# Linear attention and soft mixture of experts in one kernel: fewer and larger transfers, other homes in the arena, and two half experts moved

## Chip, cores and metric

The kernel runs on one core of a Trainium2 chip. The metric is the device time of one execution in microseconds (us); the times shown are medians of runs. TensorE does the matrix products (PE in the profile, PEld its weight loads), VectorE is DVE, ScalarE is ACT, GpSimd is POOL. SyncE (SP) issues every transfer of this kernel, on one queue that 16 DMA engines serve in the order of issue.

## What is computed

```python
kv = einsum('bhsd,bhse->bhde', k, v)              # 8 batches, 8 heads, 576 tokens, 64 wide
out = einsum('bhsd,bhde->bhse', q, kv)
x = out / sqrt(mean(out*out, -1) + 1e-6) * g_norm # 4608 tokens x 512 after the heads are joined
logits = x @ phi                                  # 4608 x 32 slots
d = softmax of logits over tokens; slot_input = d.T @ x     # 32 x 512
for e in range(8):                                # 4 slots per expert
    slot_out[e] = relu(slot_input[e] @ w1[e]) @ w2[e]       # 512 -> 1024 -> 512
return softmax of logits over slots @ slot_out    # 4608 x 512
```

All is float32. The weights w1 and w2 are 16 MB each, q, k and v 9 MB each, the result 9 MB.

## The kernel before

**Memory.** One tile, `arena`, holds all that is loaded and stored: 160 places of 256 floats for each of 128 partitions, behind a small head. `KV_AT` gives the places of k and v of each batch (18 places each), `Q_AT` those of q of each pair of batches (18), `W_AT` those of the units of w1 and w2 (16 each), `OUT_AT` those of the 12 output chunks (6 each). A place is used several times: a load into it has to wait until the last reader of what stood there is done. Unit 7 of w1 goes into `xall`, the tile that held x.

**Loads.** SP issues them in the order of the program. `load_head`, `load_row` and `load_w` are one transfer each. `W_ROWS` says which units of w1 and w2 lie side by side in memory and come in one transfer; `load_w` of a row's first member loads the row. A transfer has one completion: who needs a part of it waits for the whole. The q of pair 1 comes in two parts, `load_head(4, 0, 2048)` and `load_head(4, 2048, TOK)`.

**First stage.** `for T in range(NT - 2)` walks 36 tiles of 128 tokens, with the last two written out behind it. A batch's k and v products (`Kv.products`, line 205, `borders`, line 220) are made three steps ahead of the first tile that needs them (`kv_steps`): batch 2 at T = 6 to 8, batch 3 at T = 10 to 12, batch 4 at T = 15 to 17, batch 6 at T = 24 to 26. `products(T)` (line 273) is o = q times kv, together with its part of the logits; ScalarE squares and copies it out, VectorE, ScalarE and GpSimd make the norm and the logits, and `group_sum` (line 422) adds to the slot inputs with a running maximum. `loads_behind` names the loads that are issued behind a given T. TensorE takes all this in the order written.

**Second stage.** `fill` puts products of zeros where TensorE would otherwise stand still. Then come the experts: `expert_h(e)` (line 636) multiplies by w1, `expert_y(e, hf)` (line 654) by one half of w2's columns, so that output half 0 can leave while half 1 is still computed. Units 0 and 1 of w2 hold both halves of experts 0 and 1. For the later six, units 2, 3, 4 hold half 0 of experts 2 and 3, 4 and 5, 6 and 7, and units 5, 6, 7 half 1 of the same. `combine(k)` is the softmax over slots for a third of the tokens, on VectorE and ScalarE. `gather(hf)` copies the sum over experts from PSUM (line 670), `mix(hf)` adds its four parts by a product and copies it (z, line 676). `output(hf, k, f)` makes one of 12 chunks by four products (line 687), copied by ScalarE (line 695) and VectorE (line 697), and when the last chunk of an entry of `OUT_ROWS` is copied, SP issues that entry's transfer (line 701).

The order of half 0 and half 1 before: after `expert_h(7)`, `expert_y` of experts 2 to 7 for half 0, `gather(0)`, half of expert 0 for half 1, `mix(0)`, the other half, two chunks, experts 1 to 3, a chunk, experts 4 and 5, two chunks, experts 6 and 7, `gather(1)`, the sixth chunk, `mix(1)`, six chunks.

Of the kernel before, what the change touches and what calls it, by code (L numbers as in the profile page):

```python
# [14 lines left out]
P = 128  # L15
# [3 lines left out]
NE = 8  # L19
# [10 lines left out]
LATE_FILL = (16, 3, 3, 1, 1)  # L30
# [11 lines left out]
}  # L42
W_ROWS = (
    (("w1", 0, None), ("w2", 0, None)),
    (("w1", 1, None), ("w2", 1, None)),
    (("w1", 2, None), ("w1", 3, None)),
    (("w1", 4, None), ("w2", 2, 1)),
    (("w1", 5, None),),
    (("w1", 6, None),),
    (("w1", 7, None),),  # L50
    (("w2", 2, 0),),
    (("w2", 3, None),),
    (("w2", 4, None),),
    (("w2", 5, None),),
    (("w2", 6, None),),
    (("w2", 7, None),),
)
OUT_AT = (16, 22, 28, 34, 40, 46, 72, 128, 134, 78, 84, 90)
OUT_ROWS = ((0, 1), (2, 3), (4, 5), (6,), (7, 8), (9, 10, 11))
# [11 lines left out]
def soft_moe_linear_attention(ctx: ExitStack, tc: tile.TileContext, first_in, head_in, t2_in, kv5_in, t3_in, w_in, out):  # L71
# [13 lines left out]
    def place(at, n):  # L85
        return arena[:, HEAD + at * KB : HEAD + at * KB + n]

    def load_head(u, lo, hi):
        at = (KV_AT[0], KV_AT[1], Q_AT[0], KV_AT[2], Q_AT[1], KV_AT[3])[u]
        nc.sync.dma_start(place(at, TOK)[:, lo:hi], head_in[u, :, lo:hi])  # L90

    def load_row(at, src):
        nc.sync.dma_start(place(at, src.shape[-1]), src)
# [30 lines left out]
    def w_block(kind, u, i):  # L124
# [7 lines left out]
    load_head(0, 2304, TOK)  # L132
    load_head(2, 0, 2048)
    load_head(1, 0, 2304)
    load_head(1, 2304, TOK)
    load_head(2, 2048, TOK)
    load_head(3, 0, TOK)
    load_head(4, 0, 2048)
# [5 lines left out]
        21: lambda: load_w("w1", 1),  # L144
        26: lambda: load_w("w1", 2),
        27: lambda: load_w("w1", 4),
        31: lambda: load_w("w1", 5),
# [334 lines left out]
    load_head(5, 0, TOK)  # L482
    load_head(4, 2048, TOK)
    load_row(KV_AT[4], t2_in)
    load_row(KV_AT[5], kv5_in)
# [72 lines left out]
    load_w("w1", 6)  # L558
    load_w("w1", 7)
    load_w("w2", 2, 0)  # L560
# [151 lines left out]
    load_w("w2", 5)  # L712
    expert_y(1, 0)
    combine(1)
    for e in range(3, NE):
        expert_h(e)
        if e == 4:
            load_w("w2", 6)
            combine(2)
        if e == 5:  # L720
            load_w("w2", 7)
    for e in range(NE - LATE, NE):
        expert_y(e, 0)
    chunks = [(k, f) for k in range(NCH) for f in range(2)]
    gather(0)
    expert_y(0, 1, range(4))
    mix(0)
    expert_y(0, 1, range(4, 8))
    output(0, *chunks[0])
    output(0, *chunks[1])  # L730
    expert_y(1, 1)
    expert_y(2, 1)
    expert_y(3, 1)
    output(0, *chunks[2])
    expert_y(4, 1)
# [12 lines left out]
def build_program():  # L748
    import concourse.bacc as bacc

    nc = bacc.Bacc("TRN2", target_bir_lowering=False, num_devices=1, dynamic_dma_scratch_size=SCRATCH)
    shapes = {
        "first": (P, HEAD + 2304), "head": (6, P, TOK), "t2": (P, 2 * TOK), "kv5": (P, TOK), "t3": (P, 3 * TOK),
        "w": (1, 2 * NE * P * UNIT),
    }
    args = [nc.dram_tensor(f"in_{n}_dram", s, F32, kind="ExternalInput").ap() for n, s in shapes.items()]
    args.append(nc.dram_tensor("out_0_dram", (1, 4 * NCH * P * 4 * CT * NS), F32, kind="ExternalOutput").ap())
    with tile.TileContext(nc, schedule_with_timeline_sim=True) as tc, tc.manual_schedule():
        soft_moe_linear_attention(tc, *args)
    return nc  # L760
# [56 lines left out]
```

## Time and profile before

| | |
|---|---|
| median of three runs | 175.05 us (174.93 to 175.15) |
| the profiled execution | 175.01 us, its span 173.2 us |
| TensorE products / weight loads busy | 148.8 us / 107.2 us |
| VectorE / ScalarE / GpSimd busy | 87.2 / 87.2 / 57.2 us |
| mean granted TensorE clock | 0.967 |
| moved by all queues | 71.67 MB, mean 414 GB/s |

The span is the time from the first to the last instruction that the profile shows; the execution is 1.8 us longer. In a row of instructions the first number is the start in us from the span's beginning, the second the time taken; `x32` is the number of instructions merged into the row, and the bracket says how long the engine stood idle before and who ended that. In a row of transfers stand the KB moved and the us from issue to landing. In a row of stretches stand each engine's busy time, the granted clock, the share of the DMA engines and GB/s.

### The profile page before, as it was taken

The page shows a single profiled execution, that of the slowest core. Times are in us where ns is not written, and L with a number is a line of the kernel's source. Part 1 is how long each engine was busy: PE and PEld are TensorE (multiplying, and loading weights), DVE is VectorE, ACT ScalarE, POOL GpSimd, SP SyncE. Part 2 cuts the span into 40 slices and gives each one's busy share as a digit, 9 for nine tenths or more (in the row PEclk, how much of TensorE's full clock was granted, in tenths as well). Part 3 has the DMA queues.
Part 4 walks back from the last instruction along what each step waited for, and adds up shares of the span by engine and source line. Part 5 has one row for each costly group of instructions (what it writes and reads, how often), then busy time and mean ns, then how long its engine had stood idle before and what let it go on. Part 6 is the DMA issues. An engine that isn't in the chain of part 4 may idle for free.

```text
span 173.2 us, 4657 instructions
## 1 busy us (share of the span) xinstructions
PE 148.8 (86%) x1973; PEld 107.2 (62%) x1973; DVE 87.2 (50%) x184; ACT 87.2 (50%) x224; POOL 57.2 (33%) x68
## 2 busy tenths in 40 slices
PE   7688988999999899999999989899996499978500
PEld 2467967889689888888896773456663235433200
DVE  1112266383677464757725988526885033456600
ACT  2026586787956888869679760213221031315500
POOL 6000338558356575482765488000000000000000
PEclk9969999999999999999999999999999999999955
DMA  5999999999999998999999999999999999999994
GB/s 197 416 432 431 439 404 446 408 492 417 395 417 489 491 409 358 424 429 435 416 431 422 439 395 426 431 416 422 429 422 424 428 424 424 394 397 410 430 447 192
DMA packets 4628, 71.67 MB, mean 414 GB/s; under 512 B 512, under 2 KB 512, under 8 KB 640
## 3 DMA queue, kind: packets, MB, share of 16 engines
q1 hardware_dynamic: 4608, 71.38, 97.2%
q8 instruction: 15, 0.25, 0.6%
q14 instruction: 5, 0.04, 0.1%
HBM read 61.94 MB, written 9.44 MB: 412 GB/s over the span
## 4 chain that ended last, share of the span: by engine, by line
PE 50%; DMA 24%; ACT 7%; DVE 6%; issue 3%; SPq 2%; POOL 1%; POOLq 1%; DVEq 0%
PE o L273 19%; DMA arena<-in_head_dram 13%; DMA arena<-in_w_dram 11%; PE kvp_kv L205 8%; PE po L687 6%; PE pY L654 6%; PE pS L422 3%; PE ph L636 2%; PE o L264 2%; DVE arena L697 2%; SPq L90 1%; ACT arena L695 1%; ACT sq L283 1%; PE kvp_kv L220 1%; ACT xall L291 1%
## 5 line engine op out<-in xcount | busy, mean ns | idle before, releaser
L273 PE MATMUL o<-bd,arena 128*128 128x192 f32 x256 | 49.3, 336 | 1.9 <-ACT bd L250 1.1
L273 PEld LDWEIGHTS o<-bd,arena 128*128 128x128 f32 x256 | 40.8, 190 | 5.2 <-ACT bd L250 1.6
L296 DVE TENSOR_REDUCE ms<-sq 128x16 f32<-128x1024 f32 (+1 forms) x19 | 22.1, 1163 | 28.7 <-ACT sq L283 28.4
L323 POOL TENSOR_TENSOR xall<-xall,r 128x512 f32<-128x512 f32 x34 | 34.8, 1044 | 0.0
L345 POOL TENSOR_TENSOR part<-part,r 128x512 f32<-128x512 f32 x17 | 17.8, 1048 | 49.4 <-DVE r L314 49.4
L283 ACT ACTIVATE sq<-o 128x512 f32<-128x512 f32 x36 | 21.5, 598 | 10.9 <-PE o L273 10.5
L291 ACT COPY xall<-o 128x512 f32<-128x512 f32 x34 | 20.6, 607 | 0.0
L695 ACT COPY arena<-po 128x768 f32<-128x768 f32 x12 | 9.3, 800 | 22.0 <-PE po L687 21.9
L654 PE MATMUL pY<-arena,xall 128*32 128x256 f32 x256 | 15.8, 381 | 3.8 <-DMA arena<-in_w_dram 3.3
L205 PE MATMUL kvp_kv<-arena 128*64 128x64 f32 x480 | 17.2, 225 | 2.1 <-DMA arena<-in_first_dram 1.1
L205 PEld LDWEIGHTS kvp_kv<-arena 128*64 128x64 f32 x480 | 15.2, 138 | 5.6 <-DMA arena<-in_first_dram 2.0
L358 DVE TENSOR_REDUCE logits<-part 128x64 f32<-128x512 f32 (+1 forms) x18 | 17.8, 991 | 0.0
L697 DVE COPY arena<-po 128x768 f32<-128x768 f32 x12 | 11.3, 956 | 10.6 <-PE po L687 10.6
L687 PE MATMUL po<-logits,z 32*128 32x384 f32 x96 | 13.5, 525 | 2.1 <-DVE z L676 0.9
L654 PEld LDWEIGHTS pY<-arena,xall 128*32 128x32 f32 x256 | 8.0, 109 | 11.1 <-issue 4.8
L636 PE MATMUL ph<-arena,sTe 128*32 128x256 f32 x224 | 12.7, 379 | 0.3 <-DVE sTe L583 0.3
L290 ACT COPY part<-o 128x256 f32<-128x256 f32 x34 | 12.6, 370 | 0.0
L422 PE MATMUL pS<-xall,d 128*32 128x129 f32 x288 | 10.8, 277 | 1.2 <-ACT d L410 1.1
L687 PEld LDWEIGHTS po<-logits,z 32*128 32x128 f32 x96 | 5.8, 183 | 8.9 <-ACT arena L695 5.0
L636 PEld LDWEIGHTS ph<-arena,sTe 128*32 128x32 f32 x224 | 7.2, 110 | 5.3 <-DVE sTe L583 0.7
L422 PEld LDWEIGHTS pS<-xall,d 128*32 128x32 f32 x288 | 7.2, 109 | 4.4 <-issue 3.9
L465 PE MATMUL fill<-zeros 128*128 128x512 bf16 x26 | 8.3, 476 | 1.1 <-DVE zeros L157 1.1
(93 smaller groups left out, 139.3 us busy)
## 6 DMA issues: line engine op xcount, KB each, us to landing
arena<-in_w_dram SPq DMA_DIRECT2D x7, 2048.0 KB, 21.1
arena<-in_w_dram SPq DMA_DIRECT2D x3, 4096.0 KB, 24.7
arena<-in_t_dram SPq DMA_DIRECT2D x1, 6912.0 KB, 36.6
out_dram<-arena SPq DMA_DIRECT2D x4, 1536.0 KB, 7.1
arena<-in_head_dram SPq DMA_DIRECT2D x2, 2304.0 KB, 23.0
arena<-in_t_dram SPq DMA_DIRECT2D x1, 4608.0 KB, 36.5
arena<-in_head_dram SPq DMA_DIRECT2D x3, 1152.0 KB, 12.0
arena<-in_w_dram SPq DMA_DIRECT2D x1, 3072.0 KB, 27.9
```

The costliest lines, as they stand in the source:

```text
L205: nc.tensor.matmul(self.pkv[lo : lo + 64, w, g], lhsT=main[:, w, 1, c, lo : lo + 64], rhs=main[:, w, 0, c, lo : lo + 64], start=c == 0 and ...
L273: nc.tensor.matmul(o[:, r, :192], lhsT=q_main(2 * g + i)[:, r, at : at + P], rhs=bds[i][:, r], start=True, stop=True)
L283: nc.scalar.activation(sqs[s][:, T - starts[s]], o[:, :, 32:160], AF.Square, scale=0.125)
L291: nc.scalar.copy(xts[T % NX][:, :, :128], o[:, :, 32:160])
L296: nc.vector.tensor_reduce(out=mss[s], in_=sqs.pop(s).rearrange("p t j (w d) -> p (t j w) d", w=2), axis=AX.X, op=ALU.add)
L323: nc.gpsimd.tensor_tensor(out=x, in0=x, in1=r[:, i].rearrange("p (j w) -> p j w", w=2).unsqueeze(3).to_broadcast([P, 4, 2, D]), op=ALU.mult,)
L345: engine.tensor_tensor(out=part, in0=part, in1=rs_of[s].unsqueeze(3).to_broadcast([P, STAGES[s], H, NS]), op=ALU.mult)
L358: nc.vector.tensor_reduce(out=L[:, pos(starts[s]) : pos(starts[s]) + STAGES[s]], in_=parts.pop(s).rearrange("p t h n -> p t n h"), axis=AX ...
L422: nc.tensor.matmul(pS[32 * j : 32 * j + 32], lhsT=ds[G][:, i], rhs=x[:, j], start=i == 0, stop=i == GROUPS[G] - 1)
L636: nc.tensor.matmul(ph[32 * j : 32 * j + 32], lhsT=sTe[:, (4 * e + c) * NS : (4 * e + c + 1) * NS], rhs=w_block("w1", e, 4 * c + j), start= ...
L654: nc.tensor.matmul(pY[32 * j : 32 * j + 32, hf, :256], lhsT=hTs[e][:, c], rhs=w_block("w2", u, at + c), start=e == 0 and c < 4, stop=e == ...
L687: nc.tensor.matmul(po[:, u, : CT * NS].rearrange("p (g x) -> p g x", g=2), lhsT=z[lo : lo + 32, f * P : (f + 1) * P], rhs=cT[k][lo : lo + 32],
```

## The change

Transfers are joined and moved. The second half of the first batch's k and v, q of pair 0 and batch 1 are loaded as before. Batch 2's k and v come in one transfer with the first part of q of pair 1; the rest of q of pair 1 with batch 4's k and v; q of pair 2 with batch 5's. Units 0 and 1 of w1 become one row; units 0 and 1 of w2 join unit 4 of w1 and half 1 of unit 2 of w2 (behind T = 27); half 0 of unit 2 of w2, unit 6 and unit 5 of w1 become one row, issued where unit 6 was; units 3 and 4 of w2 one row, units 5 and 6 another. The row with units 2 and 3 of w1 moves from T = 26 to T = 25, and the row that stood ahead of it (units 1 of w1 and w2, T = 21) is gone. Unit 1 of w1, units 0, 4 and 6 of w2 and all output chunks get other homes. The seventh, eighth and ninth chunk leave in one transfer, so that outputs are five transfers and not six. In the second stage, half 1 of experts 0 and 1 is computed ahead of experts 4 to 7 of half 0, with four fill products behind it, and the chunks of half 0 are placed anew.

```diff
-LATE_FILL = (16, 3, 3, 1, 1)
+LATE_FILL = (16, 3, 3, 1, 1, 4)
...
 W_AT = {
-    ("w1", 0): (72,), ("w2", 0): (88,), ("w1", 1): (128,), ("w2", 1): (144,), ("w1", 2): (0,),
+    ("w1", 0): (72,), ("w1", 1): (88,), ("w2", 0): (128,), ("w2", 1): (144,), ("w1", 2): (0,),
     ("w1", 3): (16,), ("w1", 4): (104,), ("w1", 5): (56,), ("w1", 6): (40,), ("w1", 7): None,
-    ("w2", 2): (32, 120), ("w2", 3): (72,), ("w2", 4): (128,), ("w2", 5): (0,), ("w2", 6): (104,), ("w2", 7): (56,),
+    ("w2", 2): (32, 120), ("w2", 3): (72,), ("w2", 4): (88,), ("w2", 5): (0,), ("w2", 6): (16,), ("w2", 7): (56,),
 }
 W_ROWS = (
-    (("w1", 0, None), ("w2", 0, None)),
-    (("w1", 1, None), ("w2", 1, None)),
+    (("w1", 0, None), ("w1", 1, None)),
     (("w1", 2, None), ("w1", 3, None)),
-    (("w1", 4, None), ("w2", 2, 1)),
-    (("w1", 5, None),),
-    (("w1", 6, None),),
+    (("w1", 4, None), ("w2", 2, 1), ("w2", 0, None), ("w2", 1, None)),
+    (("w2", 2, 0), ("w1", 6, None), ("w1", 5, None)),
     (("w1", 7, None),),
-    (("w2", 2, 0),),
-    (("w2", 3, None),),
-    (("w2", 4, None),),
-    (("w2", 5, None),),
-    (("w2", 6, None),),
+    (("w2", 3, None), ("w2", 4, None)),
+    (("w2", 5, None), ("w2", 6, None)),
     (("w2", 7, None),),
 )
-OUT_AT = (16, 22, 28, 34, 40, 46, 72, 128, 134, 78, 84, 90)
-OUT_ROWS = ((0, 1), (2, 3), (4, 5), (6,), (7, 8), (9, 10, 11))
+OUT_AT = (32, 38, 44, 50, 104, 110, 116, 122, 128, 134, 140, 146)
+OUT_ROWS = ((0, 1), (2, 3), (4, 5), (6, 7, 8), (9, 10, 11))
...
     nc.sync.dma_start(arena[:, : HEAD + 2304], first_in)
-    load_head(0, 2304, TOK)
-    load_head(2, 0, 2048)
-    load_head(1, 0, 2304)
-    load_head(1, 2304, TOK)
-    load_head(2, 2048, TOK)
-    load_head(3, 0, TOK)
-    load_head(4, 0, 2048)
+    load_row(KV_AT[0] + 9, kv_in[0, :, 2304:])
+    load_row(Q_AT[0], q0_in[:, :2048])
+    load_row(KV_AT[1], kv_in[1, :, :2304])
+    load_row(KV_AT[1] + 9, kv_in[1, :, 2304:])
+    load_row(Q_AT[0] + 8, q0_in[:, 2048:])
+    load_row(KV_AT[2], kv2_in)
 
     loads_behind = {
         9: lambda: load_row(KV_AT[6], t3_in),
         18: lambda: load_w("w1", 0),
-        21: lambda: load_w("w1", 1),
-        26: lambda: load_w("w1", 2),
+        25: lambda: load_w("w1", 2),
         27: lambda: load_w("w1", 4),
-        31: lambda: load_w("w1", 5),
     }
...
-    load_head(5, 0, TOK)
-    load_head(4, 2048, TOK)
-    load_row(KV_AT[4], t2_in)
-    load_row(KV_AT[5], kv5_in)
+    load_row(KV_AT[3], kv_in[2])
+    load_row(Q_AT[1] + 8, kv4_in)
+    load_row(Q_AT[2], kv5_in)
...
-    load_w("w1", 6)
+    load_w("w2", 2, 0)
     load_w("w1", 7)
-    load_w("w2", 2, 0)
...
     expert_h(0)
+    expert_h(1)
     load_w("w2", 3)
-    expert_h(1)
-    load_w("w2", 4)
     expert_y(0, 0)
     combine(0)
     expert_h(2)
-    load_w("w2", 5)
     expert_y(1, 0)
     combine(1)
     for e in range(3, NE):
         expert_h(e)
+        if e == 3:
+            load_w("w2", 5)
         if e == 4:
-            load_w("w2", 6)
             combine(2)
         if e == 5:
             load_w("w2", 7)
-    for e in range(NE - LATE, NE):
+    expert_y(2, 0)
+    expert_y(3, 0)
+    expert_y(0, 1)
+    expert_y(1, 1)
+    fill(LATE_FILL[5], home=ps.tile([P, 2, 512], F32, tag="m", name="fill")[:, 0], cols=512)
+    for e in range(4, NE):
         expert_y(e, 0)
     chunks = [(k, f) for k in range(NCH) for f in range(2)]
     gather(0)
-    expert_y(0, 1, range(4))
     mix(0)
-    expert_y(0, 1, range(4, 8))
     output(0, *chunks[0])
     output(0, *chunks[1])
-    expert_y(1, 1)
+    output(0, *chunks[2])
     expert_y(2, 1)
     expert_y(3, 1)
-    output(0, *chunks[2])
+    output(0, *chunks[3])
     expert_y(4, 1)
     expert_y(5, 1)
-    output(0, *chunks[3])
     output(0, *chunks[4])
+    output(0, *chunks[5])
     expert_y(6, 1)
     expert_y(7, 1)
     gather(1)
-    output(0, *chunks[5])
     mix(1)
```

The inputs are laid out in memory to match the rows.

More of the change, by code (lines that the diff above doesn't have):

```diff
@@ L70, in soft_moe_linear_attention @@
 @with_exitstack
-def soft_moe_linear_attention(ctx: ExitStack, tc: tile.TileContext, first_in, head_in, t2_in, kv5_in, t3_in, w_in, out):
+def soft_moe_linear_attention(ctx: ExitStack, tc: tile.TileContext, first_in, kv_in, q0_in, kv2_in, kv4_in, kv5_in, t3_in, w_in, out):
     nc = tc.nc
@@ L86, in place @@
         return arena[:, HEAD + at * KB : HEAD + at * KB + n]
-    def load_head(u, lo, hi):
-        at = (KV_AT[0], KV_AT[1], Q_AT[0], KV_AT[2], Q_AT[1], KV_AT[3])[u]
-        nc.sync.dma_start(place(at, TOK)[:, lo:hi], head_in[u, :, lo:hi])
     def load_row(at, src):
@@ L752, in build_program @@
     shapes = {
-        "first": (P, HEAD + 2304), "head": (6, P, TOK), "t2": (P, 2 * TOK), "kv5": (P, TOK), "t3": (P, 3 * TOK),
+        "first": (P, HEAD + 2304), "kv": (3, P, TOK), "q0": (P, TOK), "kv2": (P, TOK + 2048),
+        "kv4": (P, 2560 + TOK), "kv5": (P, 2 * TOK), "t3": (P, 3 * TOK),
         "w": (1, 2 * NE * P * UNIT),
@@ L800 @@
         "in_first_dram": first,
-        "in_head_dram": np.stack([kv[0], kv[1], qm[0], kv[2], qm[1], kv[3]]),
-        "in_t2_dram": np.concatenate([kv[4], qm[2]], axis=1),
-        "in_kv5_dram": kv[5],
+        "in_kv_dram": np.stack([kv[0], kv[1], kv[3]]),
+        "in_q0_dram": qm[0],
+        "in_kv2_dram": np.concatenate([kv[2], qm[1][:, :2048]], axis=1),
+        "in_kv4_dram": np.concatenate([qm[1][:, 2048:], kv[4]], axis=1),
+        "in_kv5_dram": np.concatenate([qm[2], kv[5]], axis=1),
         "in_t3_dram": np.concatenate([kv[6], qm[3], kv[7]], axis=1),
```

## The prediction

> **What bounds the kernel now.** First the page: span, engines, transfers, queues.
>
> ```profile
> span 173.2 us, 4657 instructions
> ...
> PE 148.8 (86%) x1973; PEld 107.2 (62%) x1973; DVE 87.2 (50%) x184; ACT 87.2 (50%) x224; POOL 57.2 (33%) x68
> ...
> DMA  5999999999999998999999999999999999999994
> ...
> DMA packets 4628, 71.67 MB, mean 414 GB/s; under 512 B 512, under 2 KB 512, under 8 KB 640
> ...
> q1 hardware_dynamic: 4608, 71.38, 97.2%
> ```
>
> No engine is busy as long as the transfers. Queue q1 fills 97.2% of the span, and only the first and the last slice are not near full. The 512 small packets, 16 for each of 32 transfers, say how many transfers there are. The other 4096 are 128 rows for each. So the bound is one queue, nearly never dry, and the time is its bytes plus what each transfer costs plus any time in which it runs dry.
>
> Second, how long before its turn a transfer is issued: rows of SP (start of issue) and, for the same stretch, the time from issue to landing.
>
> ```profile
> 4.30 0.49 SPq L90 DMA_DIRECT2D arena<-in_head_dram  x1
> arena<-in_head_dram SPq DMA_DIRECT2D x1, 1024.0 KB, 24.9
> 34.30 0.33 SPq L93 DMA_DIRECT2D arena<-in_t_dram  x1
> arena<-in_t_dram SPq DMA_DIRECT2D x1, 6912.0 KB, 36.6
> 64.43 0.33 SPq L122 DMA_DIRECT2D arena<-in_w_dram  x1
> arena<-in_w_dram SPq DMA_DIRECT2D x1, 4096.0 KB, 25.9
> 76.44 0.33 SPq L122 DMA_DIRECT2D arena<-in_w_dram  x1
> arena<-in_w_dram SPq DMA_DIRECT2D x1, 4096.0 KB, 24.7
> 115.32 0.33 SPq L122 DMA_DIRECT2D arena<-in_w_dram  x1
> arena<-in_w_dram SPq DMA_DIRECT2D x1, 2048.0 KB, 15.6
> 125.68 0.33 SPq L122 DMA_DIRECT2D arena<-in_w_dram  x1
> arena<-in_w_dram SPq DMA_DIRECT2D x1, 2048.0 KB, 24.8
> 163.84 0.33 SPq L701 DMA_DIRECT2D out_dram<-arena  x1
> out_dram<-arena SPq DMA_DIRECT2D x1, 2304.0 KB, 8.6
> ```
>
> Issue plus that time is the landing: the tail of head 4 (q pair 1, first part) at 29.2, t3 at 70.9, rows `w1 1 + w2 1` at 90.3, `w1 2 + w1 3` at 101.1, unit 3 of w2 at 130.9, unit 7 at 150.5, the last output at 172.4. Each load lands 15 to 37 us after its issue, far more than its own transfer takes. The last output lands 8.6 us after its issue, and it has least in hand.
>
> Third, the chain of waits, for where TensorE waits for the queue.
>
> ```profile
> 3.81 22.82 DMA arena<-in_head_dram
> ...
> 117.05 18.80 DMA arena<-in_w_dram
> ```
>
> Two places: batch 2's k and v (kv2) land at 26.63 (issue plus length of the piece), and T=6 begins its products at 26.68 (row below); unit 4 of w2 lands at 135.85, and TensorE has waited 2.96 us (row below) for it. Between them it has little idle time, so a delay at T=6 travels to 135.
>
> **The change, part by part.**
>
> *Fewer transfers.* Loads 26 become 19, outputs 6 become 5. Price: from unit 3 (130.9) to unit 7 (150.5) four loads of 2048 KB take 19.6 us, 4.89 each; from t3 (70.9) to 90.3 two of 4096 KB take 19.4 us, 9.71 each. Two halves cost 9.78, so a join gives back 0.07. Seven give 0.49; the output join is taken as 0.03, half of that, since no row shows it: 0.52 in all, bounds 0 and 0.56. SP also issues eight times less at 0.33 us, in time it has to spare. The row `w1 2 + w1 3` took 10.8 us against 9.7; what slows it is carried unchanged.
>
> *kv2 joined with the first part of q pair 1.* The one join early in a queue that an engine is waiting for. Before, kv2 landed at 26.63 and the q part at 29.2; joined, both count as landed at 29.15. T=6 stands first in TensorE's order, everything else behind it: +2.5 us. Its idle time there becomes 0.98 + 2.5 = 3.5 us. What that does to the granted clock is read from stretches of 3.41 us, the step in which it changes here, and from the same products at two clocks:
>
> ```profile
> 4.89:8.30 3.41, 1.81 (x43) 1.48 (x43) 0.56 (x2) 0.27 (x1) 0.00 (x0) 1.00 1.01 425
> 8.30:11.71 3.41, 3.31 (x44) 2.38 (x43) 0.44 (x2) 0.52 (x2) 0.00 (x0) 0.50 1.02 429
> 25.37:28.78 3.41, 2.43 (x41) 2.07 (x40) 2.44 (x6) 2.68 (x8) 2.73 (x3) 1.00 1.07 444
> 131.18:134.59 3.41, 1.85 (x32) 1.00 (x31) 1.01 (x3) 0.47 (x1) 0.00 (x0) 1.00 1.02 432
> 134.59:138.01 3.42, 1.93 (x32) 1.13 (x32) 0.03 (x1) 0.00 (x0) 0.00 (x0) 1.00 0.99 422
> ```
>
> ```profile
> 9.20 1.98 PE L205 MATMUL kvp_o<-arena 128*64 128x64 f32 x32
> ...
> 26.68 1.15 PE L205 MATMUL kvp_kv<-arena 128*64 128x64 f32 x32 [0.98 <-DMA arena<-in_head_dram]
> ```
>
> The first number after a stretch's length is TensorE's busy time, the third from the end its clock. A stretch with 1.81 busy, mostly of narrow products (64 columns), is followed by 0.50; one with 1.85 of wider ones is not. With T=6 held to 29.15, the stretch from 25.37 keeps some 0.3 busy, far below both, so I take the next (28.78 to 32.19) at half clock. The same 32 products took 1.98 at half clock and 1.15 at full: 0.83 lost. The lower bound is 0 (these steps fall elsewhere in another execution), the upper 1.7 (half of 3.41). I take 0.9, nearest the row of the same form, which with 2.5 makes TensorE 3.4 late.
>
> The Trainium skill, "TensorE: Matmul & The Clock Gate", Part 1: The HAM clock gate, says that the clock falls after at least one idle window of some 3.4 us and that the window runs freely. Taken strictly, a wait of 3.5 us almost never holds a whole window, so that rule leaves 2.5 us late and full clock; the row with 1.81 busy ahead of a 0.50 speaks against the strict reading.
>
> *What the delay meets.* `w1 2 + w1 3` is issued behind T=25, once batch 6's borders are done, as before at 76.44: now 76.44 + 3.4 = 79.8. It had a 4096 KB row ahead of it, which is moved behind: now only `w1 0 + w1 1` stands ahead, landing at 90.3 - 9.7 - 0.14 = 80.5. Before, the slack was 90.3 - 76.4 = 14 us. From issue to landing a load needs its own transfer plus a start and a receipt. For these I take 1.3 us, midway: at least 0, at most the first load's 5.4 - 2.9 = 2.5 on an empty queue.
>
> ```profile
> 0.73 0.38 SPq L131 DMA_DIRECT2D arena<-in_first_dram  x1
> arena<-in_first_dram SPq DMA_DIRECT2D x1, 1224.0 KB, 5.4
> 101.81 0.33 SPq L122 DMA_DIRECT2D arena<-in_w_dram  x1
> ```
>
> (2.9 is 1224 KB at 4.89 for 2048.) So the queue is dry for 79.8 + 1.3 - 80.5 = 0.6 us; 0 with full clock (78.9 + 1.3 = 80.2, under 80.5), 1.4 with the upper price of the half clock. With 0 for start and receipt it is never dry at the price I take, with 2.5 it is for 1.8.
>
> The other joined rows wait for the latest home of their parts and hold back what stands behind them on SP, but keep slack: `w1 4 + w2 2 (half 1) + w2 0 + w2 1` behind T=27, some 5 us after T=25, with 10 us of transfer ahead; `w2 2 (half 0) + w1 6 + w1 5` is held by q pair 3, the release of `w1 6` before, so 101.8 + 3.4 + 1.3 = 106.5 against 80.5 + 10.8 + 17.0 = 108.3 (17.0 is 7168 KB at 9.71 for 4096); the rest is issued in the experts' stage behind 15 us of transfers. Later landings (`w2 0` some 108, `w1 5` some 121) lie ahead of their uses. The rows joined from q pair 1's rest, kv4, q pair 2 and kv5 bring kv4 earlier and go to free homes: nothing.
>
> *The tail.* It is moved from two waits into one order.
>
> ```profile
> 104.08 3.63 PE L465 MATMUL fill<-zeros 128*128 128x512 bf16 x16
> ...
> 128.89 1.91 PE L654 MATMUL pY<-arena,xall 128*32 128x256 f32 x32
> ...
> 135.99 1.93 PE L654 MATMUL pY<-arena,xall 128*32 128x256 f32 x32 [2.96 <-DMA arena<-in_w_dram]
> ...
> 140.33 1.56 PE L687 MATMUL po<-logits,z 32*128 32x384 f32 x12
> ...
> 148.43 1.56 PE L687 MATMUL po<-logits,z 32*128 32x384 f32 x12
> ...
> 151.08 1.93 PE L654 MATMUL pY<-arena,xall 128*32 128x256 f32 x32
> ...
> 155.40 1.56 PE L687 MATMUL po<-logits,z 32*128 32x384 f32 x12 [0.90 <-DVE z L676]
> ```
>
> ```profile
> 137.98 0.42 DVE L670 COPY y<-pY 128x256 f32<-128x256 f32 x1 [5.78 <-PE pY L654]
> 139.76 0.42 DVE L676 COPY z<-pz 128x256 f32<-128x256 f32 x1 [1.36 <-PE pz L674]
> ```
>
> Two experts' half takes 1.86 (32 products, less the drain of one), two chunks of output 151.08 - 148.43 = 2.65, a fill 0.22. Experts 2 and 3 start at 128.89 + 3.4 = 132.3; with experts 0 and 1 of half 1 (+1.86) and four fills (+0.9) TensorE reaches unit 3 at 132.3 + 3.72 + 0.9 = 136.9. The joined units 3 and 4 land at 135.85 - 0.42 + 0.6 = 136.0: the 2.96 us of wait are filled. Four experts take 3.8, y is copied at 140.7. From there: 0.42 copy, 0.8 for the mix (of VectorE's wait of 1.36 some 0.5 was eight products of TensorE, now moved), 0.57 from z's start to the first output product (139.76 to 140.33): 142.5. Three chunks 3.5 (2.65 and one of 8 products, 0.9 by the 12 in 1.56 less a drain), experts 2 and 3 1.86, a chunk 0.9, experts 4 and 5 1.86, two chunks 2.65, experts 6 and 7 1.86: 155.1. Again 1.8 for y, mix and z: half 1's chunks begin at 156.9, 1.5 after the 155.40 of before. The last output is issued at 163.84 + 1.5 = 165.3 and could land at 165.3 + 1.3 + 5.5 = 172.1 (5.5: 2304 KB at 4.89 for 2048). The queue lands it at 172.4 - 0.52 + 0.6 = 172.5: the queue decides, with 0.4 us to spare (with 2.5 for start and receipt the outputs do, at 173.3). Homes of the outputs (32 to 56 and 104 to 152) are read for the last time by experts 2 and 3 of half 0 and 0 and 1 of half 1, all ahead of them on TensorE: no wait.
>
> **Sum.** 175.01 (this execution; 1.8 of it lies around the span, and the median shown is 175.05) - 0.52 + 0.6 = 175.1.
>
> **The rivals.**
> *Full clock*: TensorE is 2.5 late, T=25's row arrives in time, the last output could land at 171.2, the queue's end is 171.9, and only the joins are left: 175.05 - 0.5 = 174.5. For it: those steps need not fall on the wait. Against: 0.3 busy is far under 1.81. The Trainium skill's rule on the clock window, above, taken strictly, gives this case.
> *Slower*: the half clock costs its upper price, TensorE is 4.2 late, `w1 2 + w1 3` is issued at 80.6 and the queue is dry for 1.4: 175.05 - 0.52 + 1.4 = 175.9. It decides once TensorE is more than some 3.6 late. For it: the output products that follow the 32 have no row at half clock and may take twice their time. Against: the 32 themselves lose 0.83 and not 1.15.
> *The joins give nothing back*: what differs between 4.89 x 2 and 9.71 is chance; 175.0 with a full clock, 175.7 with a dry queue. For it: the landings are read to 0.1 us. Against: the 0.07 stands in four loads against two. The Trainium skill, "DMA: Bandwidth & Descriptors", section Anatomy of one DMA, calls the bubble of the semaphore write tiny, about one cycle, which leans towards this rival; the trace, with its 0.07, neither needs nor excludes it.
>
> **How the numbers follow.** 0.2% (0.35 us) is about what can be told from no change, that is 174.7 to 175.4. Forecast 0.40 (its own range 174.7 to 175.5), full clock 0.33, slower 0.18, no gain from joins 0.09. Faster: full clock and 0.02 of the forecast, 0.35. Slower: its rival, 0.03 of the forecast and half of the last, 0.26. Same: the rest, 0.39. The range runs from 174.2, a little under full clock, to 176.2: the slower case, and the 1.2 more of dry queue that 2.5 for start and receipt would bring.
>
> **What would show it.** T=6's first product at 29.1 and not 26.7; a clock of 0.50 in the next step; the T=25 row issued near 80 and a DMA share under 1 at 80 to 82; q1 with 24 x 128 rows; no wait of about 3 us at unit 3; last issue near 165. Wrong if kv2 is not waited for, if the queue stays full at 80, or if the outputs fall behind the queue: each microsecond past 165.7 is one on the end.

## The result: 2 us slower

The changed kernel takes 177.11 us (median of four, 177.03 to 177.36) against 175.05: ratio 1.012, 95% interval 1.0103 to 1.0138. That is 2.06 us slower and above the forecast's range. A ratio leaves out executions with a lower clock and a time some per cent longer; a median counts them. The page of after, lines that answer to those of before (fortieths of the span, busy tenths and GB/s):

```profile
span 175.3 us, 4642 instructions
...
DMA  5999999999999999988999999998999999996996
GB/s 201 410 436 425 449 444 410 456 431 390 463 496 425 397 404 433 426 372 292 423 456 423 421 458 436 430 439 357 471 421 408 449 415 394 410 423 286 404 404 269
DMA packets 3476, 71.67 MB, mean 409 GB/s; under 512 B 384, under 2 KB 384, under 8 KB 384
...
q1 hardware_dynamic: 3456, 71.38, 96.0%
```

The same bytes go in 24 transfers (384 small packets, 16 each) and not 32, but the queue is full for less of a longer span: 96.0% of 175.3 us, 97.2% of 173.2 before. Where before's DMA row has 9, after's falls to 8 and 8 in slices 18 and 19 (some 75 to 83 us; 372 and 292 GB/s) and to 6 in slice 37 (some 158 to 162 us; 286). The 357 in slice 28 stands beside 471 in the next; a packet counts where it starts. By the microsecond, in stretches of after (the last two numbers are DMA share and GB/s):

```profile
19.24:22.66 3.42, 3.42 (x37) 3.19 (x32) 0.52 (x3) 0.80 (x3) 0.50 (x1) 0.50 1.04 448
...
29.48:32.90 3.42, 3.42 (x72) 3.10 (x68) 2.68 (x5) 2.52 (x8) 2.83 (x4) 1.00 1.06 448
78.00:79.00 1.00, 1.00 (x42) 0.89 (x36) 0.48 (x4) 1.00 (x5) 0.28 (x1) 1.00 0.49 205
79.00:80.00 1.00, 1.00 (x14) 0.97 (x7) 0.00 (x0) 0.71 (x2) 1.00 (x2) 1.00 0.00 0
...
161.00:162.00 1.00, 0.84 (x8) 0.36 (x8) 0.97 (x2) 0.17 (x1) 0.00 (x0) 1.00 0.26 111
```

and of before at the two places:

```profile
79.00:80.00 1.00, 1.00 (x9) 1.00 (x8) 1.00 (x2) 0.94 (x3) 0.19 (x1) 1.00 0.91 393
...
161.00:162.00 1.00, 1.00 (x10) 0.66 (x12) 0.20 (x2) 0.80 (x1) 0.00 (x0) 1.00 1.14 479
```

In after no packet starts between 79 and 80, and a quarter of the usual ones between 161 and 162. The issues beside these places, each with its time to landing (rows of SP and of the issues, after):

```profile
60.16 0.33 SPq L113 DMA_DIRECT2D arena<-in_w_dram  x1
arena<-in_w_dram SPq DMA_DIRECT2D x1, 4096.0 KB, 20.3
79.04 0.33 SPq L113 DMA_DIRECT2D arena<-in_w_dram  x1
arena<-in_w_dram SPq DMA_DIRECT2D x1, 4096.0 KB, 13.3
128.25 0.33 SPq L113 DMA_DIRECT2D arena<-in_w_dram  x1
arena<-in_w_dram SPq DMA_DIRECT2D x1, 2048.0 KB, 23.2
154.74 0.33 SPq L687 DMA_DIRECT2D out_dram<-arena  x1
out_dram<-arena SPq DMA_DIRECT2D x1, 1536.0 KB, 7.7
162.05 0.33 SPq L687 DMA_DIRECT2D out_dram<-arena  x1
out_dram<-arena SPq DMA_DIRECT2D x1, 2304.0 KB, 6.9
165.83 0.33 SPq L687 DMA_DIRECT2D out_dram<-arena  x1
out_dram<-arena SPq DMA_DIRECT2D x1, 2304.0 KB, 8.6
```

and of before, the outputs of chunks 4, 5 and of 7, 8:

```profile
155.00 0.33 SPq L701 DMA_DIRECT2D out_dram<-arena  x1
out_dram<-arena SPq DMA_DIRECT2D x1, 1536.0 KB, 6.5
160.05 0.33 SPq L701 DMA_DIRECT2D out_dram<-arena  x1
out_dram<-arena SPq DMA_DIRECT2D x1, 1536.0 KB, 6.9
```

Issue plus time gives the landings, and their difference says where the loss arose:

| landing of | before | after | difference |
|---|---|---|---|
| unit 7 of w2 | 150.5 | 151.45 | +0.95 |
| chunks 4, 5 | 161.5 | 162.4 | +0.9 |
| chunk 8 | 166.95 | 168.95 | +2.0 |
| last output | 172.4 | 174.4 | +2.0 |

So the loss comes in two steps. Up to unit 7 it is 0.95. The dry place at 79 cost more than that: the row behind T=27 lands at 83.32 + 26.5 = 109.8, and the same bytes had landed in before at 80.72 + 27.9 = 108.6, which is 1.2 earlier. With the 0.5 that the joins up to unit 7 should have given back, it is about 1.4. From chunk 5 to chunk 8 it grows by 1.1: the joined output is issued at 162.05, when chunks 4 and 5 are landing.

TensorE's rows of after, at kv2 and in the tail:

```profile
29.28 0.92 PE L193 MATMUL kvp_kv<-arena 128*64 128x64 f32 x24 [0.56 <-DMA arena<-in_kv_dram]
...
136.75 3.66 PE L640 MATMUL pY<-arena,xall 128*32 128x256 f32 x64 [0.68 <-DMA arena<-in_w_dram]
...
157.39 0.93 PE L673 MATMUL po<-logits,z 32*128 32x384 f32 x8 [0.61 <-DVE z L662]
```

### The profile page after: what moved, and what is told of

Same layout as the page of the kernel before. It is cut to its first block, busy times and chain, and to the rows that moved or that the text cites. A ratio compares the mean times of both kernels' runs of the same rounds, so it can differ in the third digit from the quotient of the medians.

```text
span 175.3 us, 4642 instructions
## 1 busy us (share of the span) xinstructions
PE 149.8 (85%) x1977; PEld 108.6 (62%) x1977; DVE 87.2 (50%) x184; ACT 87.1 (50%) x224; POOL 57.1 (33%) x68
## 4 chain that ended last, share of the span: by engine, by line
PE 49%; DMA 27%; ACT 7%; DVE 5%; issue 3%; SPq 2%; POOL 1%; POOLq 1%; DVEq 0%
PE o L261 19%; DMA arena<-in_kv_dram 15%; DMA arena<-in_w_dram 12%; PE kvp_kv L193 7%; PE pY L640 4%; PE po L673 4%; PE ph L622 4%; PE pS L410 3%; PE o L252 2%; DVE arena L683 2%; SPq L84 1%; ACT sq L271 1%; PE kvp_kv L208 1%; ACT xall L279 1%; ACT bd L228 1%
## 5 line engine op out<-in xcount | busy, mean ns | idle before, releaser
L261 PE MATMUL o<-bd,arena 128*128 128x192 f32 x256 | 50.5, 341 | 1.7 <-ACT bd L238 1.1
L261 PEld LDWEIGHTS o<-bd,arena 128*128 128x128 f32 x256 | 41.9, 194 | 5.1 <-ACT bd L238 1.6
L284 DVE TENSOR_REDUCE ms<-sq 128x16 f32<-128x1024 f32 (+1 forms) x19 | 22.1, 1162 | 29.4 <-ACT sq L271 29.1
L640 PE MATMUL pY<-arena,xall 128*32 128x256 f32 x256 | 15.2, 380 | 1.3 <-DMA arena<-in_w_dram 1.3
L673 PE MATMUL po<-logits,z 32*128 32x384 f32 x96 | 13.3, 524 | 2.3 <-DVE z L662 1.2
L410 PE MATMUL pS<-xall,d 128*32 128x129 f32 x288 | 10.8, 277 | 1.2 <-ACT d L398 1.1
L453 PE MATMUL fill<-zeros 128*128 128x512 bf16 x30 | 9.1, 456 | 1.1 <-DVE zeros L145 1.1
## 6 DMA issues: line engine op xcount, KB each, us to landing
arena<-in_w_dram SPq DMA_DIRECT2D x1, 7168.0 KB, 26.5
```

Source lines behind the costliest of these rows:

```text
L261: nc.tensor.matmul(o[:, r, :192], lhsT=q_main(2 * g + i)[:, r, at : at + P], rhs=bds[i][:, r], start=True, stop=True)
L284: nc.vector.tensor_reduce(out=mss[s], in_=sqs.pop(s).rearrange("p t j (w d) -> p (t j w) d", w=2), axis=AX.X, op=ALU.add)
L410: nc.tensor.matmul(pS[32 * j : 32 * j + 32], lhsT=ds[G][:, i], rhs=x[:, j], start=i == 0, stop=i == GROUPS[G] - 1)
L640: nc.tensor.matmul(pY[32 * j : 32 * j + 32, hf, :256], lhsT=hTs[e][:, c], rhs=w_block("w2", u, at + c), start=e == 0 and c < 4, stop=e == ...
L673: nc.tensor.matmul(po[:, u, : CT * NS].rearrange("p (g x) -> p g x", g=2), lhsT=z[lo : lo + 32, f * P : (f + 1) * P], rhs=cT[k][lo : lo + 32],
```

## The experiments

All ran beside the kernel before, which had medians of 175.0 to 175.3 there. Where a profile is quoted it is one execution. Where the times of a kernel fall in two groups, its median lies in one of them while the ratio weighs both, so both are given. "Cushion" below means a weight row that already stands in the queue when the next issue comes late.

### The joined output

First, the kernel after with chunk 6 by itself again.

```diff
-OUT_ROWS = ((0, 1), (2, 3), (4, 5), (6, 7, 8), (9, 10, 11))
+OUT_ROWS = ((0, 1), (2, 3), (4, 5), (6,), (7, 8), (9, 10, 11))
```

> The changed kernel with the seventh chunk's output back in a transfer of its own (outputs 6 / 7, 8 / 9, 10, 11). Theory: of the 2.06 us lost, 1.1 is the queue standing dry at 161, because the joined output of chunks 6, 7, 8 is issued at 162.05, when the queue has only 0.4 us left; split, chunk 6 leaves some 2.5 us sooner and the queue stays full: 177.1 - 1.1 = 176.0. Rival (TensorE's own lateness sets the end, the last output is issued at 165.83 whatever the others do): 177.1.

Measured 176.27 (ratio to before 1.0058, 1.0036 to 1.0079): 0.84 less than after by the medians, 1.1 by the ratios, and near the expected 176.0. Its queue at the place where after's was dry:

```profile
161.00:162.00 1.00, 0.77 (x8) 0.36 (x8) 1.00 (x2) 0.23 (x1) 0.00 (x0) 1.00 1.01 418
```

The other way round, the kernel before with the three chunks joined:

```diff
-OUT_AT = (16, 22, 28, 34, 40, 46, 72, 128, 134, 78, 84, 90)
-OUT_ROWS = ((0, 1), (2, 3), (4, 5), (6,), (7, 8), (9, 10, 11))
+OUT_AT = (16, 22, 28, 34, 40, 46, 128, 134, 140, 78, 84, 90)
+OUT_ROWS = ((0, 1), (2, 3), (4, 5), (6, 7, 8), (9, 10, 11))
```

> The kernel before with the outputs of chunks 6, 7, 8 in one transfer (homes moved so that they lie side by side) and nothing else. Theory: issued at 160.05, when the queue has 1.5 us left; that is about what an issue needs to reach the queue, so 0 to 0.4 us: 175.1 to 175.4. Rival (a join gives 0.03 and costs nothing): 175.0; and the other way, that it costs the 1.1 us that it costs in the changed kernel by itself: 176.1.

Measured 176.44, above the expected 175.1 to 175.4, and in two groups: five at 174.94 to 175.30 and six at 176.41 to 176.67 (ratio 1.0024, 0.999 to 1.0058). The profiled execution is of the upper group (176.67). TensorE at unit 4, the clock there, and the joined output:

```profile
132.47:135.88 3.41, 0.48 (x15) 0.05 (x5) 0.05 (x1) 0.00 (x0) 0.00 (x0) 1.00 1.05 447
135.88:139.29 3.41, 3.41 (x32) 1.60 (x32) 0.00 (x0) 0.00 (x0) 0.00 (x0) 0.50 0.96 408
...
135.86 3.60 PE L654 MATMUL pY<-arena,xall 128*32 128x256 f32 x32 [2.93 <-DMA arena<-in_w_dram]
...
161.61 0.33 SPq L701 DMA_DIRECT2D out_dram<-arena  x1
out_dram<-arena SPq DMA_DIRECT2D x1, 2304.0 KB, 6.9
```

The wait for unit 4 is the one of before (2.93 and 2.96), but here a clock step holds nearly all of it, with 0.48 busy, and the next is at half clock: 3.60 for products that took 1.93. TensorE is 1.7 later, and the joined output comes after the queue has gone dry. In this profile, then, the joined chunks leave no slack for that step. That the lower group are the executions without it is not shown: none of them was profiled, and the mean clock does not tell the groups apart (0.956 to 0.968 in the lower, 0.966 to 0.970 in the upper; before has one step at half clock too, at 8.30, where it costs nothing). The kernel before is above 176.2 as well now and then, in some one of twelve executions beside these runs.

### The kv2 join and the cushion

The kernel before with kv2 and q's first part in one load, all else kept:

```diff
-    load_head(3, 0, TOK)
-    load_head(4, 0, 2048)
+    load_row(KV_AT[2], kv2_in)
```

> The kernel before with one part of the change alone: batch 2's k and v joined with the first part of q of pair 1. Theory: TensorE is 2.5 us late from T=6 on, but the T=25 row has 14 us of transfers ahead of it, and the lateness ends in the wait of 2.96 us for unit 4 of w2: 175.0. Rival (lateness reaches the end): 176.5 to 177.5.

Measured 175.02 (0.9989, 0.9967 to 1.0011). TensorE does wait:

```profile
29.05 1.15 PE L204 MATMUL kvp_kv<-arena 128*64 128x64 f32 x32 [1.33 <-DMA arena<-in_kv_dram]
...
135.69 1.93 PE L653 MATMUL pY<-arena,xall 128*32 128x256 f32 x32 [0.71 <-DMA arena<-in_w_dram]
```

T=6 starts 2.4 us later than before, and the delay is gone at unit 4, where the wait shrinks from 2.96 to 0.71. Then the same without the cushion ahead of the rows of T=26 and T=27:

```diff
-        21: lambda: load_w("w1", 1),
-        27: lambda: load_w("w1", 4),
+        27: lambda: (load_w("w1", 4), load_w("w1", 1)),
```

> The kernel before with the kv2 join, and the row w1 1 + w2 1 issued behind T=27 and no longer behind T=21, so that the T=25 row (here T=26) has only one row ahead of it. Theory: the queue stands dry for 1.1 to 1.4 us near 80, and that reaches the end: 176.2. Rival (the dry stretch is taken up later, as the other outputs wait for data anyway): 175.0.

Measured 176.62 (1.0082, 1.0048 to 1.0116): the delay and the missing cushion together cost 1.6 us. The missing cushion without the delay was not tried in the kernel before.

In the kernel after, the two parts were undone in turn. kv2 and q apart:

```diff
-    load_row(KV_AT[2], kv2_in)
+    load_row(KV_AT[2], kv2_in[:, :TOK])
+    load_row(Q_AT[1], kv2_in[:, TOK:])
```

> The changed kernel with batch 2's k and v and the first part of q of pair 1 in two transfers again. Theory: T=6 begins at 26.7 again, the T=25 row is issued at 76.4, the queue does not run dry at 80 and units 3 and 4 land at 135.4; TensorE gets there at 134.3 and waits, so the tail is 1.1 us earlier and no more, and the queue still stands dry for chunks 6, 7, 8: 176.0. Rival (2.5 us late on TensorE pass in full to the end): 177.1 - 2.5 = 174.6.

Measured 177.11 (1.0102, 1.0065 to 1.0139), and not 176.0: no gain that shows in an interval of this width. With chunk 6 by itself as well (this edit and the first one):

> The changed kernel with both splits: six joins are left. Theory: neither dry stretch, so the queue's end is that of before less six joins of 0.07: 175.05 - 0.42 = 174.6. Rival (the larger rows are themselves slower, or TensorE's order decides): 175.4 to 176.

Measured 176.22 (1.0054, 1.0031 to 1.0077), 175.23 to 177.3: the same as with chunk 6 alone. In its profiled execution (175.46) the place at 79 is full:

```profile
79.00:80.00 1.00, 1.00 (x9) 1.00 (x8) 1.00 (x1) 0.96 (x3) 0.48 (x1) 1.00 0.96 393
```

The row behind T=25 goes out at 76.73 there, and the row behind T=27 lands at 108.6 as in before. So bringing TensorE 2.4 us forward does fill that place, and yet the median does not fall. Now a cushion instead, `w2 0 + w2 1` as a row of its own behind T=21:

```diff
-    (("w1", 4, None), ("w2", 2, 1), ("w2", 0, None), ("w2", 1, None)),
+    (("w1", 4, None), ("w2", 2, 1)),
+    (("w2", 0, None), ("w2", 1, None)),
...
+        21: lambda: load_w("w2", 0),
```

> The changed kernel with units 0 and 1 of w2 as a row of their own behind T=21, so that 4096 KB more stand in the queue ahead of the T=25 row; kv2 stays joined. Theory: no dry stretch at 80 although TensorE is 2.6 us late; units 3 and 4 land near 135.3, TensorE reaches them at 136.1 and goes on 0.65 us sooner than in the changed kernel; chunks 6, 7, 8 still leave late: 176.4. Rival (the 10.4 to 11.9 us that the T=25 row takes is its own, not a dry queue): 177.2.

Measured 177.55 (1.0103, 1.0069 to 1.0138), not 176.4. In its profile the first place is full, and the second has grown:

```profile
161.00:162.00 1.00, 0.64 (x6) 0.34 (x8) 1.00 (x2) 0.66 (x1) 0.00 (x0) 1.00 0.06 25
162.00:163.00 1.00, 1.00 (x12) 0.31 (x6) 0.79 (x2) 0.38 (x1) 0.00 (x0) 1.00 0.00 0
...
162.54 0.33 SPq L689 DMA_DIRECT2D out_dram<-arena  x1
out_dram<-arena SPq DMA_DIRECT2D x1, 2304.0 KB, 6.9
```

The joined output is issued 0.5 later than in after and lands 6.9 after its issue, as there. What the cushion wins is gone before it: the row behind T=27 lands at 108.9 (109.8 in after), but unit 7 of w1 at 127.4 (126.9), and units 3 and 4 of w2 at 137.1 (136.6). In the trace fifteen of the 16 DMA engines complete that unit 7 by 125.9; one alone is 1.5 behind. So the cushion and chunk 6 by itself together (both edits as above):

> The changed kernel with units 0 and 1 of w2 as a row of their own behind T=21 (so the queue has 4096 KB more ahead of the T=25 row) and the seventh chunk's output in a transfer of its own; kv2 stays joined, TensorE 2.6 us late. Theory: no dry stretch at 80 and none at 161, so the lateness costs nothing by itself: 175.05 - 0.35 = 174.7, up to 175.2 where one DMA engine is held longer. Rival (TensorE's lateness at T=6 reaches the end however the queue is filled): 176 to 177.

Measured 176.0 (1.0032, 1.0006 to 1.0059), 175.11 to 176.65: better than the cushion alone, little better than chunk 6 alone (1.0058), and still 0.9 above before by the medians, 0.6 by the ratio. With kv2 and q apart too (three edits as above):

> As the run before, and batch 2's k and v in a transfer of their own too: the changed kernel with three of its joins undone. Theory: 174.7, the same as with kv2 joined. Rival (lateness at T=6 counts): 1 to 2 us faster than the run before. A second rival: TensorE now reaches units 3 and 4 some 2 us before their joined transfer, stands still there and goes on at half clock for 3.4 us: 175.5 to 176.5.

Measured 175.36 (1.000, 0.9974 to 1.0026): the time of before. The two intervals overlap, but the step hints at a third place that minds TensorE's delay.

### What it was not

The order of experts and chunks, with the four fills, in the kernel before (the last part of the change's diff alone, from `expert_y(2, 0)` to `mix(1)`, and `LATE_FILL`):

```diff
-    for e in range(NE - LATE, NE):
+    expert_y(2, 0)
+    expert_y(3, 0)
+    expert_y(0, 1)
+    expert_y(1, 1)
+    fill(LATE_FILL[5], home=ps.tile([P, 2, 512], F32, tag="m", name="fill")[:, 0], cols=512)
+    for e in range(4, NE):
         expert_y(e, 0)
...
```

> The kernel before with the order of experts and chunks of the changed kernel, and its four fills, and nothing else. Theory: half 1 of experts 0 and 1 fits into the wait of 2.96 us for unit 4, y of half 0 is copied near 138 as before, the outputs are no later, and the queue sets the end: 175.0. Rival (the order is what costs): 175.7 to 176.

Measured 174.96 (0.9983, 0.9963 to 1.0003): it costs nothing. Units 3 to 6 of w2 in four transfers, in the kernel after with cushion and chunk 6 by itself:

```diff
-    (("w2", 3, None), ("w2", 4, None)),
-    (("w2", 5, None), ("w2", 6, None)),
+    (("w2", 3, None),),
+    (("w2", 4, None),),
+    (("w2", 5, None),),
+    (("w2", 6, None),),
...
+    load_w("w2", 4)
...
+            load_w("w2", 6)
```

> The changed kernel with the row of 4096 KB behind T=21 again, chunk 6's output apart, and units 3, 4, 5, 6 of w2 in four transfers again; kv2 and the other early rows stay joined, and the order of the experts is the changed one. Theory: what is left of the loss in the run with the first two repairs (176.0) is that TensorE waits for unit 4 before it may use unit 3, and for unit 6 before unit 5, so that y, z and all outputs are later and the queue has no slack at the end; apart, experts 4 and 5 begin near 135 and not 136, and the end is the queue's: 174.8. Rival (the new order of experts and chunks costs it): 175.7 to 176.

Measured 176.23 (1.0047, 1.0016 to 1.0079): nothing gained, so these joins are not the third place. A first try at a better version, the kernel before with all joins up to the middle (kv2; kv4 with q 1's rest; kv5 with q 2; `w2 2 half 0 + w1 6 + w1 5`; the diffs of the three follow or stand above):

> The kernel before with four joins for which nothing waits: kv2 with q of pair 1, its rest with batch 4, q of pair 2 with batch 5, and half 0 of unit 2 of w2 with units 6 and 5 of w1 (two joins). Theory: five transfers less at 0.07 each: 175.05 - 0.3 = 174.7 to 174.8, faster than the kernel before by little. Rival (a join gives nothing back): 175.05.

Measured 176.69 (1.0079, 1.0047 to 1.011): 1.7 above the kv2 join alone. This held the third place, and the next four runs looked for it.

### The late joined row

The kv2 join, and of the rest only the weight row:

```diff
-    (("w1", 5, None),),
-    (("w1", 6, None),),
-    (("w2", 2, 0),),
+    (("w2", 2, 0), ("w1", 6, None), ("w1", 5, None)),
...
-        31: lambda: load_w("w1", 5),
...
-    load_w("w1", 6)
+    load_w("w2", 2, 0)
     load_w("w1", 7)
-    load_w("w2", 2, 0)
```

> The kernel before with the joined kv2 load and, of the weights, the one row `w2 2 half 0 + w1 6 + w1 5` in place of three loads, issued where `w1 6` was; the loads of kv4 and kv5 stay as before. Theory (this row is issued just as the queue runs out, so its first packets are slow and all behind it comes later, the last output with it): 176.4 to 176.8, with the row issued near 104.2 and landing near 122. Rival (the joined kv4 and kv5 loads are what costs, by holding TensorE up early): 175.0. Rival (joins give their 0.07 each): 174.9.

Measured 176.72 (1.01, 1.0082 to 1.0118). The other half of that version, the kv2 join with the kv4 and kv5 joins:

```diff
-    load_head(4, 2048, TOK)
-    load_row(KV_AT[4], t2_in)
-    load_row(KV_AT[5], kv5_in)
+    load_row(Q_AT[1] + 8, kv4_in)
+    load_row(Q_AT[2], kv5_in)
```

> The kernel before with the joined kv2 load and the joined loads of kv4 with the rest of q 1 and of kv5 with q 2; all weight rows as before. Theory (the late weight row is what costs): 174.9 to 175.0. Rival (the joined kv4 and kv5 loads hold TensorE up early and cost through the clock or later issues): 176.4 to 176.8.

Measured 174.85 (0.9988, 0.9974 to 1.0003): harmless. And the row taken apart in the kernel after that has a cushion and chunk 6 by itself:

```diff
-    (("w2", 2, 0), ("w1", 6, None), ("w1", 5, None)),
+    (("w1", 5, None),),
+    (("w1", 6, None),),
+    (("w2", 2, 0),),
...
+        31: lambda: load_w("w1", 5),
...
+    load_w("w1", 6)
+    load_w("w1", 7)
     load_w("w2", 2, 0)
-    load_w("w1", 7)
```

> The kernel after with `w2 0 + w2 1` as a row of its own behind T=21, chunk 6 put out by itself, and `w1 5`, `w1 6`, `w2 2 half 0` as three loads at the places that they had before (the first behind T=31). Theory (what is left of the loss in the version without this last edit, 176.0, is the late weight row): 174.8 to 175.1. Rival (what is left is the joined kv2 load together with a step of half clock): 175.9 to 176.2.

Measured 175.0 (1.0004, 0.9989 to 1.0019): the whole loss of the change is gone. The rows show how the join makes the load late. First the kernel before with the kv2 join, `w1 5`, `w1 6` and unit 7:

```profile
90.05 0.33 SPq L122 DMA_DIRECT2D arena<-in_w_dram  x1
arena<-in_w_dram SPq DMA_DIRECT2D x1, 2048.0 KB, 23.2
104.17 0.33 SPq L122 DMA_DIRECT2D arena<-in_w_dram  x1
arena<-in_w_dram SPq DMA_DIRECT2D x1, 2048.0 KB, 14.0
...
128.05 0.33 SPq L122 DMA_DIRECT2D arena<-in_w_dram  x1
arena<-in_w_dram SPq DMA_DIRECT2D x1, 2048.0 KB, 22.2
```

and with the joined row, that row and unit 7:

```profile
104.28 0.33 SPq L120 DMA_DIRECT2D arena<-in_w_dram  x1
arena<-in_w_dram SPq DMA_DIRECT2D x1, 5120.0 KB, 18.4
...
128.15 0.33 SPq L120 DMA_DIRECT2D arena<-in_w_dram  x1
arena<-in_w_dram SPq DMA_DIRECT2D x1, 2048.0 KB, 23.9
```

The other loads from 60 us on are issued within 0.13 us of the same time, but `w1 5` alone went out at 90 and joined it goes out at 104, with the last of the three homes to come free. Unit 7 lands at 152.05 and not at 150.25. In the trace's packets the row's first ones start at 105.25, 0.97 after the issue, on DMA engines that have run out, and several take 0.4 to 1.1 us longer than the usual 1.51; the row lands 14.3 us after the one ahead of it, against 12.1 for its bytes. One DMA engine makes the difference: fifteen complete the row by 120.6 and unit 7 by 150.2 (in the version without the join all 16 complete unit 7 by 150.2), and the last is 2.1 and 1.9 behind them. TensorE waits for the last.

Is it the lateness or the size? Two runs, both on the kernel before with the kv2 join. `w1 5` moved in the program to the place of `w1 6`, four loads kept:

```diff
-        31: lambda: load_w("w1", 5),
...
+    load_w("w1", 5)
     load_w("w1", 6)
```

> The kernel before with the joined kv2 load, and `w1 5` issued not behind T=31 but with `w1 6` and `w1 7`, about 14 us later; `w1 5`, `w1 6`, `w1 7` and `w2 2 half 0` stay four loads. Theory (late issue: the queue runs out near 104 and the first packets of what comes next are slow): 176.4 to 176.8. Rival (what costs is the size of the joined row, 40 KB for each partition): 174.9 to 175.1.

Measured 174.96 (0.9981, 0.9967 to 0.9996). This didn't test what it was meant to: `w1 5` was not issued later.

```profile
91.83 0.33 SPq L122 DMA_DIRECT2D arena<-in_w_dram  x1
arena<-in_w_dram SPq DMA_DIRECT2D x1, 2048.0 KB, 21.8
```

SP issues it 14.1 us ahead of `w1 6` (105.93), as far as in the version without the move (90.05 and 104.17): what holds a load is its home's release, not its line. And `w2 2 half 0` joined to `w1 6`, with `w1 5` left alone:

```diff
-    (("w1", 6, None),),
+    (("w2", 2, 0), ("w1", 6, None)),
...
-    (("w2", 2, 0),),
```

> The kernel before with the joined kv2 load; `w1 5` stays behind T=31, and `w2 2 half 0` and `w1 6` are joined to one load at the place of `w1 6`. Theory (late issue): 174.9 to 175.1. Rival (the size of a joined row, here 24 KB for each partition): 175.4 to 176.2.

Measured 174.97 (0.9988, 0.9978 to 0.9999): this join, of 3072 KB and behind an early `w1 5`, costs nothing. On size, two more profiles help. After has the same row of 5120 KB, and so has the version with kv2 apart, chunk 6 by itself and the cushion.

```profile
104.39 0.33 SPq L113 DMA_DIRECT2D arena<-in_w_dram  x1
arena<-in_w_dram SPq DMA_DIRECT2D x1, 5120.0 KB, 17.6
```

```profile
102.29 0.33 SPq L114 DMA_DIRECT2D arena<-in_w_dram  x1
arena<-in_w_dram SPq DMA_DIRECT2D x1, 5120.0 KB, 18.7
```

In after it finds the queue still full, because the dry place at 79 has already made the queue 1.2 late (first packet at 107.16); in the second it is issued 2 us earlier. In both it lands 12.1 after the row ahead. So the same size is harmless with work ahead of it; three loads all issued late but apart were not tried. Nor does lateness cost in every execution. In the profiles of the cushion alone, of the cushion with chunk 6 and of that with the units apart, the row is issued at 104.38, 104.43 and 104.31 and its first seven packets take 1.7 to 2.7 us, yet it lands only 12.15 to 12.40 after the row ahead. That it costs where slow packets fall on the DMA engine that is already last would fit, and is not tested. The times of the last two versions run from 175.0 to 176.7 in all but two executions.

Last, the two harmless parts of the change together (kv2 join and order) in the kernel before:

> The kernel before with the joined kv2 load and with the order of experts and chunks of after (both halves of experts 0 and 1 ahead of unit 4), outputs of chunk 6 and of chunks 7 and 8 apart. Both parts by themselves left the time where it was. Theory (the queue sets the end, nothing is late): 174.9. Rival (the fuller wait keeps the clock at the end, and it wins): 174.5.

Measured 175.21 (1.001, 0.9984 to 1.0037): no gain. No version beat the kernel before by more than about 0.2%; the lowest medians, 174.85 to 175.02, all belong to versions with every cushion in place.

## Why the prediction was wrong

*The step that failed: the tail.* It asked of the last output alone whether it could land before the queue's end (0.4 us to spare) and never of the joined output ahead of it. By its own numbers, chunks of half 1 start 1.5 us later, so chunk 8 is issued at 160.05 + 1.5 = 161.6, while chunks 4 and 5 land at 161.5 + 0.1 = 161.6; with 1.3 us for start and receipt the queue is dry for 1.3 there, and chunk 6, which used to fill it, waits for chunk 8. Measured: issue 162.05, 1.1 lost; 0.84 by the medians and 1.1 by the ratios came back with chunk 6 by itself. This term was missing from the sum and from the rivals.

*The term mis-sized: the dry queue at 80, 0.6 us.* Measured 1.2 to 1.4. TensorE's part came out smaller than forecast: the row behind T=25 was issued at 79.04, not 79.8, and by the prediction's formula (79.04 + 1.3 against 80.5) the queue wouldn't have run dry at all. Two of its inputs were wrong. The end of the work ahead was read from a landing (80.5), which is that of the slowest of 16 DMA engines: between 78 and 79 only half the usual packets start and then none, so most engines had nothing left by then. And start and receipt were taken as 1.3. From issue to landing the row took 13.3 us, 3.6 more than its own 9.7. Of these, 1.1 stood in before's row too (10.8), which the prediction carried unchanged; the 2.5 that are left are its upper bound. So the rival "full clock" had the right delay of TensorE (2.6 us) and still not its 174.5, and the slower rival named the right place, with 175.9 for it, for a reason that didn't occur.

*The clock.* The half step was put at 28.78 to 32.19, behind the wait for kv2. In after it fell at 19.24 to 22.66, and its delay was swallowed by the wait (0.56 left of it), so the 0.9 us was not paid. It can be: in the version with `w1 5` moved, whose program up to there is that of the kv2 join alone, the step at half clock runs from 29.57 to 32.98, and the row behind T=26 goes out at 80.59, against 78.81 in the profile of the kv2 join, which has no such step. That is 1.8 us, twice the price taken and just above its upper bound. What the prediction had as "these steps fall elsewhere in another execution" decides between the two.

*Slack taken as safe.* For the row `w2 2 half 0 + w1 6 + w1 5` it found 106.5 against 108.3 and "keep slack". In after that held (12.1 us from landing to landing), with a queue that was already late; with the other two places mended the row cost 1.0 by the medians (176.0 against 175.0) and 0.5 by the ratios, and in the kernel before 1.7. Its 108.3 was again a landing of the slowest engine, while the first engines were out at 105.

*Right, in part by luck.* T=6 at 29.15 (measured 29.28, and 29.05 in the kernel before with that join); half 1's chunks at 156.9 (157.39), last issue 165.3 (165.83). TensorE at unit 3 at 136.9 (136.75) is luck: it was to arrive there after units 3 and 4 had landed (136.0). It arrived at 136.07, as the half clock was not paid, and waited 0.68 for a load that landed at 136.6, as the queue was later than forecast. "Each microsecond past 165.7 is one on the end" was hardly tried: the last issue was 0.13 past it and the end 2.0 later, by the queue. The order is harmless by itself. The 0.07 us for a join, 0.5 for all, enters the 1.4 above as the prediction had it; no run shows it in a total: the kernel after with cushion, chunk 6 and the late row mended has 28 transfers to before's 32 and takes the same time. Two readings are off without weight: "15 to 37 us" from issue to landing holds for the rows shown and not for each load (the first took 5.4), and its own terms put the top of the range at 175.1 + 1.2 = 176.3.

*Sum as measured:* 175.05 + 0.95 (to unit 7: the dry place less the joins) + 1.1 (joined output) = 177.1, against 177.11. Both steps are read from the same two profiles, so the sum agrees by its making. Undone one at a time, the parts do not add: the cushion alone gave nothing, and each mended place uncovered another. With all three mended the loss is gone, which shows that they are its cause together. The joined output's share is clear, since the intervals of after and of the version with chunk 6 by itself stand apart; how the rest divides is less sure, since those of the further steps overlap. What stays open: why kv2 apart gave nothing in the kernel after with and without chunk 6 apart, although its profile shows the place at 79 filled and it gives 0.6 with the cushion.

## What to carry to other kernels

In a kernel that one DMA queue bounds, check every transfer's issue against the end of the work ahead of it, not the last one's alone, and ask for 3 to 4 us of slack by landings. That is an estimate: the engines were 2 to 3.5 us apart here, and a load that met engines just run out began some 1.0 after its issue. A join saves 0.07 us by the landings and nothing that a total showed, and it issues all its parts when the last one's home (or data) is ready: at best it pays where all are ready anyway. When one dry place is mended and nothing is gained, look for the next one behind it before dropping the explanation.

## What the runs showed of the hardware

- A landing is set by the slowest of the 16 DMA engines. The trace's packets point to why one is slow: 15 packets of 16 KB on q8, the instruction queue, take some 1.07 us each. In before the first two start at 17.22 and 26.62; of the 16 completions of a load, one then comes 1.1 after the rest (21.1 against 20.0), and later two (29.1 and 29.2 against 28.0). The slowest engine is 2 us behind the first by 80 us and 3.5 by 120, in a queue that never drains; where after's had run dry, all 16 complete the joined output within 0.2. The Trainium skill, "DMA: Bandwidth & Descriptors", section Anatomy of one DMA, puts the fixed cost of a transfer at about 2.0 us, most of it the receipt (on GpSimd's path). Here the joined output of after took 6.9 us on a drained queue, where its bytes take some 5.5 (2304 KB at the 4.89 of 2048 KB): 1.4 beyond them, less than that figure. The row at 79.04, whose way ahead was not quite clear, took 3.6 beyond its bytes.
- The clock falls also after a step that is not wholly idle (0.48 of 3.41 busy), and whether a wait of 2.9 us brings it down differs between executions: not in the profile of before, but in that of before with the joined output. The Trainium skill, "TensorE: Matmul & The Clock Gate", Part 1: The HAM clock gate, says that the window runs freely and that the point of change moves with it. The two profiles agree with that; it has the clock fall after at least one idle window, which is stricter than what they show.
